# Three more steps of hp in seven products, in chunk 1, and what is moved to make room for them

## The chip, the cores and the metric

The kernel runs on one core of one Trainium2 chip. The metric is the device time of one execution, in microseconds. The core's engines work side by side, each through its own list of instructions in order, and wait for each other through semaphores: TensorE (PE, matrix products into PSUM), VectorE (DVE), ScalarE (ACT), GpSimd (POOL), and SyncE (SP), which starts most of the DMA transfers.

## The reference

Two blocks follow each other. The first is a chunked scan (Mamba-2's SSD) over 4 sequences of 8 heads and 768 positions; the second is a feed-forward layer over the 3072 tokens that come out of it.

```python
# scan: batch 4, heads 8, seq 768, head_dim 32, d_state 16
la = np.log(np.clip(a, 1e-06, 1.0))
for c in range(nc):                         # chunks of positions
    cum = np.cumsum(la[chunk c], axis=-1)
    L = np.exp(cum[..., :, None] - cum[..., None, :]) * causal
    M = np.einsum('bhin,bhjn->bhij', Cc, Bc) * L
    y = np.einsum('bhij,bhjd->bhid', M, xc) \
        + np.einsum('bhin,bhnd->bhid', Cc, state) * np.exp(cum)[..., None]
    state = np.exp(np.sum(la))[..., None, None] * state \
        + np.sum(Bc outer xc * np.exp(cum[..., -1:] - cum), axis=positions)
# feed-forward: x is y as (3072 tokens, 256)
h = x @ w_in                                # 256 -> 2048
g = h * np.cos(h)
out = g @ w_out                             # 2048 -> 256
```

## The kernel before, in words

All data are float32. The 768 positions are cut into NC = 6 chunks of 128 positions; a chunk has 4 x 128 = 512 tokens. The feed-forward layer of chunk c is cut into NF = 16 steps, so that there are 96 steps, n = 16 c + f. A step takes 256 of the 512 tokens (a unit, u = 0 or 1) and 256 of the 2048 features. In step n

- `first(n)` writes hp = x w_in of the step, 512 columns of one PSUM bank, by four products of 128x128 weights with 256 columns (L662);
- `wind_k` (ScalarE, L669) and `wind_w` (VectorE, L675) reduce hp to a fraction of a turn, `gate` (ScalarE, L684) takes the cosine, and `gated` (VectorE, L689) writes gT = hp cos(hp). gT is the last reader of hp;
- from chunk 1 on `differ` (GpSimd, L714, L716, L717) forms the differences gd of gT's four blocks;
- `second(n - 2)` adds the step of two before to the output o. In chunks 1 to 5 that is `seven` (L838): a product of 2x2 blocks by seven block products with 128 columns in place of eight, whose seven sums are taken apart once a unit is through (`rest`, L863, from ps, the copy of o).

`first7` does for hp what `seven` does for o: seven products (L762) in place of four of twice the width. It needs differences of y on GpSimd (`differ_y`, L744, four of them, into the scratch tile ms[2]) and of w_in (`differ_in`, L733, four tiles wid), a copy on ScalarE (L769), and four sums on VectorE (L775, L778, L780, L783). The products are issued in the order 1, 6, 7, 5, 4, 3, 2; product 6 reads the third difference of y, product 4 the fourth. The steps that are done so stand in `runs`: before the change f = 9 to 13 of chunks 2, 3 and 4, and 13 steps of chunk 5. In a run, VectorE and ScalarE work on a step while TensorE makes the next (`late`), and `first_of_seven` picks the PSUM bank of hp:

```python
if i == 0:
    at_["hp"] = pair("hp")[:, 0]
    at_["m"] = pair("m").rearrange("p b (q m) -> p b q m", m=P)
to_ = at_["hp"] if i % 3 == (n > NF * (NC - 1)) else bank([P, TB], "hp", "h")
```

Here i counts the steps of the run, and the step behind the run is counted too. m holds the sums of products that are not in hp's own blocks.

PSUM has 8 banks: two buffers of one bank for "o", two for "h" (hp), and two buffers of two banks each, which `pair` hands out in turn: to the products of C and B (g), to y, and in a run to hp and m. A new holder of a buffer waits until the last reader of the old one is done.

Between the steps of chunk c the scan of chunk c + 1 is made, its parts placed by hand in `steps`, by f: `reach` (running products, L576), `turn` (transposes of B and C on VectorE, L584, then in the next step cT on ScalarE, L593, and rT on VectorE, L595), `inner` (`inner2`: products of C and B into the two g, L605), `weigh` (`weights`: g by the decays lam, on VectorE, L467, which frees g), `state` (`add_state`: the state over a sub-chunk, VectorE, L500), `decays` (running products lam, VectorE, L377, and at the end of each pair sc, GpSimd, L383) and `along` (loads). `open2(c + 1)` multiplies C by the state into two new y tiles (L619) and forms sums (L479); `finish2` adds the products of x (L631) at the end of the chunk. For chunk 2, which is prepared in chunk 1, the places differ from those of the others, since the first chunks are done in another form. There, `add_s` (L553, L560) forms the last state of chunk 1 in that form, and `exchange` (L565) moves quarters of it with four DMAs on SP's queue.

The order of instructions on each engine is the order in which the program issues them; nothing reorders them. In step n it is, in short: hp of step n; on VectorE w of the step; GpSimd's and VectorE's work for the scan; gT; `open2` where it is due; o of step n - 2; `inner2`.

Of the kernel before, what the change touches and what calls it, by code (L numbers as in the profile page):

```python
# [25 lines left out]
def kernel(  # L26
# [18 lines left out]
    NC = S // P  # L45
    DM, DF = moe_w_in.shape
    KT = DM // P
    NF = DF // P
# [23 lines left out]
    def pair(name):  # L72

        return psum.tile([P, 2, 4 * P], FP32, tag="scan", bufs=2, name=name)


    along, blocks = {}, {}
# [54 lines left out]
    def group(q, s):  # L132
        return slice(32 * (q ^ s), 32 * (q ^ s) + 32)
# [223 lines left out]
    reach, part, yT, after = {}, {}, {}, {}  # L357
# [71 lines left out]
    def reach_unit(k):  # L429

        flat = "p b i -> p (b i)"
        V.tensor_tensor_scan(
            out=reachs[k].rearrange(flat), data0=alongs[k].rearrange(flat),
            data1=lead.rearrange(flat), initial=0.0, op0=ALU.mult, op1=ALU.add)
# [35 lines left out]
    def sums(k, at, strip, start=False):  # L470

        sc = scs.pop(k).rearrange("p (q k h) n -> p q k (h n)", q=2, h=2)
        x2 = xrs[k].rearrange("p q (k h) d -> p q k (h d)", h=2)
        for p in range(2):
            for s in range(2):
                ss = slice(s * W, (s + 1) * W)
                for q in range(4):
                    r = strip(q, s)
                    PE.matmul(at[s][r, p * W:(p + 1) * W], lhsT=sc[ss, p, q], rhs=x2[ss, p, q],  # L479
                              start=(start and p == 0), stop=True,  # L480
                              tile_position=(s * W, r.start), skip_group_check=True)
# [131 lines left out]
    def open2(c):  # L613

        ys[c] = y = [pair("y") for _ in range(2)]
        for k, p, s, q in ((k, p, s, q) for k in range(2) for p in range(2) for s in range(2)
                           for q in range(4)):
            r, o_, i = group(q, s), W * (q % 2), (2 * k + p) * W
            PE.matmul(y[s][o_:o_ + W, q // 2, i:i + W], lhsT=after[2 * c + k - 1][r, s, p],  # L619
                      rhs=part[c, s][2][r, p, k * W:(k + 1) * W], start=(k == p == 0), stop=False,  # L620
                      tile_position=(r.start, o_), skip_group_check=True)
        for k in range(2 if c < NC - 1 else 0):
            sums(2 * c + 1 + k, [y[s][:, 0, (2 + k) * P:(3 + k) * P] for s in range(2)], group)
# [21 lines left out]
    NJ = NF // 2  # L645
# [52 lines left out]
    def differ_w(i, js):  # L698

        if i == len(wd):  # L700
            t = conv.tile([P, 2 * WC, 2], U32, tag="words", bufs=8, name="words")
            wd.append(t.rearrange("p a w -> p (a w)").bitcast(FP32)
                      .rearrange("p (j m) -> p j m", j=NJ))
        w11, w12, w21, w22 = (w4[:, js, e, h] for e in range(2) for h in range(2))
        a_ = (w12, w22, w22, w21)[i]
        b_ = (w11, w12, wd[0][:, js], wd[min(i, 2)][:, js])[i]
        op = ALU.add if i in (1, 2) else ALU.subtract
        G.tensor_tensor(out=wd[i][:, js], in0=a_, in1=b_, op=op)  # L708
# [15 lines left out]
    def differ_in(i, js):  # L724

        if i == len(wid):
            t = conv.tile([P, 2 * WC, 2], U32, tag="words", bufs=8, name="wid")
            wid.append(t.rearrange("p a w -> p (a w)").bitcast(FP32)
                       .rearrange("p (j f) -> p j f", j=NJ))
        g = [win4[:, k, js, e] for k in range(2) for e in range(2)]  # L730
        a_ = (g[1], g[1], g[0], g[2])[i]
        b_ = (g[3], g[0], wid[0][:, js], wid[min(i, 2)][:, js])[i]
        G.tensor_tensor(out=wid[i][:, js], in0=a_, in1=b_, op=ALU.subtract)  # L733

    def differ_y(c, i, eng, us=slice(0, 2)):

        if i == 0:
            yd[c] = ms[2].rearrange("p (i u m) -> p i u m", i=4, u=2)
        d = yd[c]
        y11, y12, y21, y22 = (yT[c][:, us, k, h * P:(h + 1) * P] for k in range(2)  # L740
                              for h in range(2))
        a_ = (y12, y22, y22, y21)[i]
        b_ = (y11, y12, d[:, 0, us], d[:, 2, us])[i]
        eng.tensor_tensor(out=d[:, i, us], in0=a_, in1=b_,  # L744
                          op=ALU.add if i in (1, 2) else ALU.subtract)
# [125 lines left out]
    unsummed, finished, summed = [], [], [0]  # L871
# [96 lines left out]
    def rest_of_loads():  # L968
# [21 lines left out]
        for k in (4, 5):  # L990
            for s in range(2):
# [1 line left out]

    steps = {c: dict(reach=(5, 6), turn=(6, 7), inner=8, weigh=(9, 10), state=(-NF, 12),
                     decays=(8, 11, 13, 14), along=(12, 13)) if c == 2 else
             dict(reach=(1, 2), turn=(3, 4), inner=5, weigh=(6, 7), state=(0, 5),
                  decays=(2, 8, 14, 15), along=(6, 7)) for c in range(2, NC)}
    first_decays = (NF + 1, NF + 2, NF + 3, NF + 4)  # L1000
# [11 lines left out]
    def decays2(k, p):  # L1012
        decays0(k, p)
        if p == 1:
# [8 lines left out]

    runs = [*(range(NF * c + 9, NF * c + 14) for c in range(2, NC - 1)),
            range(NC * NF - 15, NC * NF - 2)]
    sevens = {n: r for r in runs for n in r}
    late, at_ = [], {}
# [76 lines left out]
    for n in range(AHEAD, NC * NF + LAG):  # L1106
        c, f = divmod(n, NF)
        if n < NC * NF:
# [64 lines left out]
            if add_s and (n == NF - 5 or units_at(n - 1, 4)):  # L1173
                exchange = add_s()
                add_s = None
            if n == NF + 9:
                exchange()
            for do in behind:
                do()
            if n == runs[-1][0] - 2:  # L1180
                for i in range(4):
                    differ_y(NC - 1, i, V)
            for i, at in enumerate((4, 5, 6, 6) if 2 <= c < NC - 1 else ()):
                if at == f:
                    differ_y(c, i, G, slice(1, 2))
            if unsummed and (c > 1 or summed[0]):
                unsummed[0](range(summed[0], summed[0] + 1), G)
                summed[0] = (summed[0] + 1) % 4
                if summed[0] == 0:
                    unsummed.pop()  # L1190
            elif n not in sevens and f not in ((10, 11, 12) if c == 1 else (10, 11)):
                for do in unsummed:
                    do()
                unsummed.clear()
# [2 lines left out]
                    weigh0(k)  # L1197
        for i, js in differ_at.get(n, ()):
            differ_w(i, js)
        for start, js in zip((2 * NF - 5, 3 * NF - 3, 4 * NF - 3),  # L1200
                             (slice(1, 6), slice(0, 1), slice(6, NJ))):
            if start <= n < start + 4:
                differ_in(n - start, js)
        if f == NF - 2 and 1 < c < NC - 1:
            open2(c + 1)
        if n == AHEAD + 1:
            second(AHEAD - LAG)
# [4 lines left out]
        for k in units_at(n, 3):  # L1212
            for t in range(2):
                inner(k, t)
            if k == 3:
                at = [gs[k, s][:, 0, 2 * P:] for s in range(2)]
# [5 lines left out]
            take_s()  # L1222
        for k in units_at(n, 1):
            reach_unit(k)
        if n == 2 * NF - 3:
            open2(2)
        for at, e in block_loads.items():
            if at == n:
                loading = load_blocks(e)
# [32 lines left out]
```

## Time and profile before

| | |
|---|---|
| runs | 364.67, 366.04, 367.22 us; median 366.04 us |
| the profiled execution | 365.45 us, of it 363.7 us from its first to its last instruction (the span) |
| TensorE | busy 357.1 us (98% of the span), 4070 matmuls, granted clock 1.00 |
| its weight loads | busy 326.1 us (90%) |
| VectorE | busy 275.4 us (76%) |
| GpSimd | busy 237.5 us (65%) |
| ScalarE | busy 184.2 us (51%) |
| the chain that ended last | 92% on TensorE, 3% GpSimd, 2% DMA |

A line of the profile names the source line, the engine, the operation, and the tiles as output<-inputs. In the timeline the first two numbers of a row are its start and its length in microseconds, equal operations that follow each other are merged into one row (x8), and what stands in square brackets at the end is idle time before the row and what ended it. Every float32 product is two matmul instructions. Matmuls overlap, so the time that one costs is read from the starts of rows that follow each other, not from their lengths. The times of the runs and of the profiled execution hold some 2 us that lie outside the span.

### The profile page before, as it was taken

The page shows a single profiled execution, that of the slowest core. Times are in us where ns is not written, and L with a number is a line of the kernel's source. Part 1 is how long each engine was busy: PE and PEld are TensorE (multiplying, and loading weights), DVE is VectorE, ACT ScalarE, POOL GpSimd, SP SyncE. Part 2 cuts the span into 40 slices and gives each one's busy share as a digit, 9 for nine tenths or more (in the row PEclk, how much of TensorE's full clock was granted, in tenths as well). Part 3 has the DMA queues.
Part 4 walks back from the last instruction along what each step waited for, and adds up shares of the span by engine and source line. Part 5 has one row for each costly group of instructions (what it writes and reads, how often), then busy time and mean ns, then how long its engine had stood idle before and what let it go on. Part 6 is the DMA issues. An engine that isn't in the chain of part 4 may idle for free.

```text
span 363.7 us, 10280 instructions
## 1 busy us (share of the span) xinstructions
PE 357.1 (98%) x4070; PEld 326.1 (90%) x4070; DVE 275.4 (76%) x504; ACT 184.2 (51%) x352; POOL 237.5 (65%) x387
## 2 busy tenths in 40 slices
PE   8999999999999999999999999999999999999995
PEld 4688888889899999999989999999999999999995
DVE  7779998478777986877766877775766775688774
ACT  3497656544464345544446543545553544454542
POOL 5557776679757787575685565686666565475562
PEclk9999999999999999999999999999999999999999
DMA  7996947693666427311417202110001001001001
GB/s 138 251 358 151 186 109 120 88 155 58 127 102 90 92 52 115 47 31 45 84 40 123 31 5 67 34 33 13 0 2 31 0 3 32 0 3 31 2 14 46
DMA packets 97328, 26.43 MB, mean 73 GB/s; under 512 B 87328, under 2 KB 93184, under 8 KB 97280
## 3 DMA queue, kind: packets, MB, share of 16 engines
q1 hardware_dynamic: 96032, 25.38, 34.9%
q8 instruction: 32, 0.52, 0.7%
q10 hardware_dynamic: 1248, 0.39, 0.5%
q14 instruction: 16, 0.13, 0.1%
HBM read 22.36 MB, written 3.34 MB: 71 GB/s over the span
## 4 chain that ended last, share of the span: by engine, by line
PE 92%; POOL 3%; DMA 2%; DVE 1%; issue 1%; ACT 0%; POOLq 0%; DVEq 0%; ACTq 0%
PE o L838 34%; PE hp L662 31%; PE m L762 7%; PE o L798 7%; PE hp L762 5%; DMA bc<-in_C_dram 2%; PE y L631 2%; PE g L605 1%; PE y L479 1%; PE y L619 1%; POOL gd L714 1%; PE g L458 1%; POOL words L708 1%; PE y L527 1%; PE y L517 1%
## 5 line engine op out<-in xcount | busy, mean ns | idle before, releaser
L662 PE MATMUL hp<-yT,w_in 128*128 128x256 f32 x544 | 129.5, 382 | 0.1
L662 PEld LDWEIGHTS hp<-yT,w_in 128*128 128x128 f32 x544 | 99.0, 190 | 13.7 <-issue 1.3
L714 POOL TENSOR_TENSOR gd<-gT 128x256 f32<-128x256 f32 x79 | 58.9, 745 | 76.4 <-DVE gT L689 64.2
L684 ACT ACTIVATE w<-w,quarter 128x512 f32<-128x512 f32 x96 | 69.4, 723 | 65.0 <-DVE w L675 64.8
L675 DVE SCALAR_TENSOR_TENSOR w<-hp,k 128x512 f32<-128x512 f32 x96 | 65.7, 685 | 46.6 <-ACT k L669 46.4
L669 ACT ACTIVATE k<-hp 128x512 int32<-128x512 f32 x96 | 57.1, 595 | 69.8 <-PE hp L662 61.0
L689 DVE TENSOR_TENSOR gT<-hp,w 128x512 f32<-128x512 f32 x96 | 65.5, 682 | 11.9 <-ACT w L684 7.4
L838 PE MATMUL o<-words,gd 128*128 128x128 f32 x474 | 66.1, 276 | 0.1
L838 PEld LDWEIGHTS o<-words,gd 128*128 128x128 f32 x474 | 59.3, 192 | 0.3 <-POOL gd L716 0.3
L838 PE MATMUL o<-w_out,gT 128*128 128x128 f32 x316 | 50.3, 278 | 0.0
L838 PEld LDWEIGHTS o<-w_out,gT 128*128 128x128 f32 x316 | 45.4, 191 | 3.1
L716 POOL TENSOR_TENSOR gd<-gT,gd 128x128 f32<-128x128 f32 x79 | 40.5, 512 | 6.2
L717 POOL TENSOR_TENSOR gd<-gT,gd 128x128 f32<-128x128 f32 x79 | 37.3, 472 | 6.2
L838 PE MATMUL o<-w_out,gd 128*128 128x128 f32 x158 | 30.6, 276 | 0.0
L838 PE MATMUL o<-words,gT 128*128 128x128 f32 x158 | 30.5, 275 | 0.0
L798 PE MATMUL o<-w_out,gT 128*128 128x256 f32 x128 | 30.0, 380 | 0.0
L377 DVE TENSOR_TENSOR_SCAN lam<-arow,unit 128x512 f32<-128x512 f32 x20 | 29.6, 1480 | 0.0
L798 PEld LDWEIGHTS o<-w_out,gT 128*128 128x128 f32 x128 | 24.2, 190 | 3.6 <-POOL w_out L273 0.4
L838 PEld LDWEIGHTS o<-words,gT 128*128 128x128 f32 x158 | 24.0, 192 | 0.0
L838 PEld LDWEIGHTS o<-w_out,gd 128*128 128x128 f32 x158 | 24.0, 192 | 0.0
L762 PE MATMUL m<-m,wid 128*128 128x128 f32 x168 | 23.5, 276 | 0.0
L762 PE MATMUL hp<-yT,w_in 128*128 128x128 f32 x112 | 21.6, 275 | 0.0
(130 smaller groups left out, 460.8 us busy)
## 6 DMA issues: line engine op xcount, KB each, us to landing
words<-in_moe_w_in_dram SPq DMA_DIRECT2D x8, 512.0 KB
words<-in_moe_w_out_dram SPq DMA_DIRECT2D x8, 512.0 KB
xr<-in_x_dram SPq DMA_DIRECT2D x24, 128.0 KB
arow<-a_cut SPq DMA_DIRECT2D x10, 256.0 KB
arow<-a_cut SPq DMA_DIRECT2D x10, 252.0 KB
out_dram<-sum SPq DMA_DIRECT2D x18, 128.0 KB
bc<-in_B_dram SPq DMA_DIRECT2D x24, 64.0 KB
blocks<-in_B_dram SPq DMA_DIRECT2D x16, 32.0 KB
```

Of the source, the lines that this page charges most:

```text
L377: V.tensor_tensor_scan(out=lams[k][:, p, hs].rearrange(flat), data0=rows_.rearrange(flat), data1=unit0[:, hs].rearrange(flat), initial=0.0 ...
L662: PE.matmul(to_[:, e], lhsT=w_in[:, k, fs], rhs=y[:, k], start=(k == 0), stop=(k == KT - 1), skip_group_check=True)
L669: ACT.activation(k, hp[n], AF.Copy, bias=0.25, scale=INV_2PI)
L675: V.scalar_tensor_tensor(out=w, in0=hp[n], scalar=INV_2PI, in1=k, op0=ALU.mult, op1=ALU.subtract)
L684: ACT.activation(cos, cos, AF.Sin, bias=quarter, scale=TWO_PI)
L689: V.tensor_tensor(out=gT[n], in0=hp.pop(n), in1=cos, op=ALU.mult)
L714: G.tensor_tensor(out=d[:, 0:2], in0=g[:, 1:2].to_broadcast([P, 2, P]), in1=g[:, 3::-3], op=ALU.subtract)
L716: G.tensor_tensor(out=d[:, 2], in0=g[:, 0], in1=d[:, 0], op=ALU.subtract)
L717: G.tensor_tensor(out=d[:, 3], in0=g[:, 2], in1=d[:, 2], op=ALU.subtract)
L762: PE.matmul(dst[q], lhsT=w[q], rhs=y_[q], start=(q in (6, 1, 7)), stop=True, skip_group_check=True)
L798: PE.matmul(o[c, u][:, t], lhsT=g[:, 2 * e + t], rhs=w_out[:, 2 * j + e], start=(j == e == t == 0), stop=(j == NJ - 1 and e == 1), skip_gr ...
L838: PE.matmul(at[q], lhsT=a_[q], rhs=w[q], start=(j == 0 and q in starts), stop=(j == NJ - 1), skip_group_check=True)
```

## The change

- `runs` gets a run of three steps in chunk 1: n = 27, 28, 29 (f = 11 to 13). The four differences of y of chunk 1 are formed on GpSimd in steps 24, 25 and 26 (f = 8, 9, 10, 10).
- The differences of w_in, which all stood behind step 26, are cut otherwise: columns 3 to 5 in steps 22, 22, 24 and 25; 1 and 2 in steps 30 to 33; 0 and 6 to 7 as before.
- `open2(2)`, the state times C, moves from the end of step 29 (behind o of step 27) to step 30, between hp of step 30 and o of step 28, where the other chunks have it.
- The sums of unit 0 of chunk 1 (L863), which were four operations on VectorE in one step, become one on GpSimd in each step of the run and the one behind it.
- In `steps` of chunk 2: `state` (-16, 12) becomes (-16, 10), and `decays` (8, 11, 13, 14) becomes (7, 8, 14, 15). With the decays, the loads of arow and sc (L383) that hang on them move.
- `exchange()` moves from step 25 to step 24.

```diff
-    steps = {c: dict(reach=(5, 6), turn=(6, 7), inner=8, weigh=(9, 10), state=(-NF, 12),
-                     decays=(8, 11, 13, 14), along=(12, 13)) if c == 2 else
+    steps = {c: dict(reach=(5, 6), turn=(6, 7), inner=8, weigh=(9, 10), state=(-NF, 10),
+                     decays=(7, 8, 14, 15), along=(12, 13)) if c == 2 else
...
-    runs = [*(range(NF * c + 9, NF * c + 14) for c in range(2, NC - 1)),
+    runs = [range(NF + 11, NF + 14), *(range(NF * c + 9, NF * c + 14) for c in range(2, NC - 1)),
             range(NC * NF - 15, NC * NF - 2)]
...
-            if n == NF + 9:
+            if n == NF + 8:
                 exchange()
...
-            for i, at in enumerate((4, 5, 6, 6) if 2 <= c < NC - 1 else ()):
+            for i, at in enumerate((8, 9, 10, 10) if c == 1 else (4, 5, 6, 6) if 2 <= c < NC - 1
+                                   else ()):
                 if at == f:
                     differ_y(c, i, G, slice(1, 2))
-            if unsummed and (c > 1 or summed[0]):
+            if unsummed and (c > 1 or n in sevens or summed[0]):
                 unsummed[0](range(summed[0], summed[0] + 1), G)
...
-        for start, js in zip((2 * NF - 5, 3 * NF - 3, 4 * NF - 3),
-                             (slice(1, 6), slice(0, 1), slice(6, NJ))):
-            if start <= n < start + 4:
-                differ_in(n - start, js)
-        if f == NF - 2 and 1 < c < NC - 1:
+        for at, js in (((22, 22, 24, 25), slice(3, 6)), ((30, 31, 32, 33), slice(1, 3)),
+                       ((45, 46, 47, 48), slice(0, 1)), ((61, 62, 63, 64), slice(6, NJ))):
+            for i, m in enumerate(at):
+                if m == n:
+                    differ_in(i, js)
+        if f == NF - 2 and 1 <= c < NC - 1:
             open2(c + 1)
...
-        if n == 2 * NF - 3:
-            open2(2)
```

## The prediction

> **What bounds the kernel now.** I read the engine totals and the chain that ended last first, then the timeline engine by engine round the edited steps, and last the same steps of the next chunk, which already run in the new form.
>
> ```profile
> PE 357.1 (98%) x4070; PEld 326.1 (90%) x4070; DVE 275.4 (76%) x504; ACT 184.2 (51%) x352; POOL 237.5 (65%) x387
> PE 92%; POOL 3%; DMA 2%; DVE 1%; issue 1%; ACT 0%; POOLq 0%; DVEq 0%; ACTq 0%
> ```
>
> TensorE is busy for 357.1 of 363.7 us and is 92% of the chain. No stage has slack to give back: a microsecond in which TensorE waits is a microsecond at the end, and one that it saves is gained only if nobody else is late.
>
> The TensorE timeline of steps 27 to 30 (chunk 1), and then of two seven-product steps and step 46 (chunk 2):
>
> ```profile
> 115.54 1.89 PE L662 MATMUL hp<-yT,w_in 128*128 128x256 f32 x8
> 117.27 0.61 PE L838 MATMUL o<-w_out,gT 128*128 128x128 f32 x4
> ...
> 118.83 1.89 PE L662 MATMUL hp<-yT,w_in 128*128 128x256 f32 x8
> ...
> 125.51 0.94 PE L619 MATMUL y<-rT,state 32*64 32x64 f32 x64
> ...
> 176.01 0.39 PE L762 MATMUL hp<-yT,w_in 128*128 128x128 f32 x2
> ...
> 179.14 0.39 PE L762 MATMUL hp<-yT,w_in 128*128 128x128 f32 x2
> ...
> 182.26 1.89 PE L662 MATMUL hp<-yT,w_in 128*128 128x256 f32 x8
> 184.09 0.91 PE L619 MATMUL y<-rT,state 32*64 32x64 f32 x64
> ```
>
> The reader sees that hp by four products costs 1.73 us (115.54 to 117.27) of a step of 3.29 (115.54 to 118.83), that a step with seven products lasts 3.13 (176.01 to 179.14), and that in chunk 2 the state products (L619) follow the hp of step 46 without idle.
>
> VectorE behind that hp of step 46, and GpSimd ahead of step 25:
>
> ```profile
> 186.07 0.68 DVE L675 SCALAR_TENSOR_TENSOR w<-hp,k 128x512 f32<-128x512 f32 x1
> 186.67 1.44 DVE L377 TENSOR_TENSOR_SCAN lam<-arow,unit 128x512 f32<-128x512 f32 x1
> 188.03 0.66 DVE L689 TENSOR_TENSOR gT<-hp,w 128x512 f32<-128x512 f32 x1
> ...
> 112.34 0.73 POOL L714 TENSOR_TENSOR gd<-gT 128x256 f32<-128x256 f32 x1
> ```
>
> gT of step 46 is done at 188.69, 4.6 us after TensorE was through with that step's hp at 184.09. Nobody waits for it there. GpSimd begins gd of step 24 at 112.34.
>
> **What the edit saves.** Steps 27, 28 and 29 take 3.13 instead of 3.29 us: 3 x 0.16 = **-0.5 us**. That is all it can bring. The sums of unit 0 leave VectorE (127.49 to 130.99 before, L863), where nothing on TensorE's path waited for them, and become four GpSimd operations of 0.73, 0.73, 0.73 and 0.46 us (the rows from 175.33 on), each behind a gd, with 0.6 us and more idle after it in chunk 2: 0. The three L769 copies (0.27 each) and three times four VectorE sums (0.29, 0.41, 0.43, 0.29) fit as they do in chunk 2: 0, and uncovered 1.7 us a step.
>
> **A wait at step 30: the state products.** `pair` hands out two PSUM buffers in turn. After the change they go to the two g of step 24, then to hp and m of the run (step 27), then to the two y of `open2`, which now stands behind hp of step 30 and ahead of o of step 28. `first_of_seven` puts hp into the pair's bank whenever i % 3 is 0. With five steps in a run (chunks 2 to 4) that is f = 9 and 12, long consumed at f = 14. With three steps it is step 27 and, as i = 3, step 30 itself. So the second y takes the buffer in which hp of step 30 has just been written, and in the built program its first product waits for VectorE's count after gT of step 30, hp's last reader. Before gT come k, w, cos on ScalarE and VectorE, those of step 29 ahead of them, and the lam scan of step 30, which stands between w and gT as in step 46. The nearest row is therefore step 46 itself: 188.69 - 184.09 = **+4.6 us** in which TensorE has nothing in front of it but the rest of `open2`; o of step 28 and hp of step 31 are queued behind. Low end: step 25, whose k, w and cos find their engines free: hp ends at 110.69 (108.86 + 1.83), gT at 113.82 (113.13 + 0.69), 3.1. High end: the scan collides with GpSimd as at 131.59, where it took 2.45 instead of 1.37 us: 4.6 + 1.1 = 5.7.
>
> ```profile
> 131.41 1.56 POOL L733 TENSOR_TENSOR wid<-w_in,wid 128x640 f32<-128x640 f32 x1
> ...
> 131.59 2.45 DVE L377 TENSOR_TENSOR_SCAN lam<-arow,unit 128x512 f32<-128x512 f32 x1
> ```
>
> **A wait at step 27: the differences of y.** The second product of step 27 (q = 6) needs the third difference of `differ_y`, on GpSimd in step 26. From 112.34 on GpSimd's order is now: sc of L383, moved here from 120.22 (0.64); gd of step 24 (112.34 to 114.11, 1.77); a difference of y (0.46, 0.5 with the gap); wid of 384 columns (between 0.73 for 256 and 1.54 for 640, a line through them gives 1.0, with gap 1.05); gd of step 25 (1.8); y (0.5); wid (1.05); y (0.5), the one that is needed. Sum 7.8, so 120.1. Without a wait the product would start at 115.54 + 0.22 = 115.76: 4.4 late. GpSimd may reach this chain sooner, since gT of step 23 now runs ahead of the transposes (0.7), and L717 of that step, 1.25 us at 108.87 beside the scan, may take its usual 0.46: 1.5 together, so 2.9 late. I take **+3.8**, nearer to the row as it stands, because the scan still meets GpSimd, with another operation. The two wid operations put into step 22 (2.1 us) fall into GpSimd's idle time of 104.11 to 107.46.
>
> VectorE gives the floor. The scan and gT of step 23 (108.40 to 110.40, 2.0 us) now stand ahead of the transposes, of which the second used to wait for its DMA until 106.14. So the transposes end at about 107.7 instead of 106.80, cT on ScalarE is 0.9 later, and the products of `inner2`, which began on it at 107.78, wait as long. Hp of step 26 and w follow 0.9 later, and the two `weights` that free the g buffers now run together behind w of step 26 (114.87 before): 114.87 + 0.9 + 0.6 + 2 x 0.6 = 117.6, 1.8 after 115.76. These waits run beside GpSimd's, so they are not added but are the low end: +1.8. If they ran one behind the other, 0.9 + 4.4 = 5.3.
>
> The exchange (L565) is issued a step earlier and `add_state` two steps earlier. L560 ended at 112.39 before and `add_state` begins near 118, so the four transfers of 16 KB have some 5 us; SP's queue has two arow loads ahead of them that wait for nothing late. `add_state` (four L500, 2.37 us) now lies between `weights` and the sums of step 27, inside TensorE's wait: 0, and 2.4 if that wait is gone.
>
> **Clock.** A gap of 4.6 us is longer than any that this trace has between matmuls (the longest after the first 10 us is 0.74). After the last matmul, which ended at 359.9, the granted clock is still 1.00 in the last row, up to 363.7:
>
> ```profile
> 362.00:363.70 1.70, 0.00 (x0) 0.00 (x0) 0.00 (x0) 0.00 (x0) 0.00 (x0) 1.00 0.08 18
> ```
>
> So 3.8 us of idleness did not lower it. (The columns are the stretch, its length, the busy time of the five engines, the granted clock, and two of DMA.) What a lowered clock would cost is bounded by the kernel's start:
>
> ```profile
> 3.46 2.56 PE L366 MATMUL a_ps<-m 128*128 128x256 f32 x6
> ```
>
> A pass of 256 columns took 0.43 us there (2.56 / 6) against 0.22 later, for about 5 us: half of that, 2.5. I take 0, with 2.5 as the high end. [...]
>
> **Sum.** -0.5 + 4.6 + 3.8 = +7.9. The profiled execution took 365.45 us (span 363.7), so 373.35; the median of the runs, 366.04, lies 0.6 above it. I say 373.5.
>
> **Rivals.** (1) *GpSimd keeps up*, and step 27 waits for VectorE alone: 365.45 - 0.5 + 4.6 + 1.8 = 371.35. For it: 1.5 us of GpSimd's delays may go, and VectorE's part is bounded; against it: 7.8 us of GpSimd work in a row. (2) *The clock falls* in the gap of step 30: 373.4 + 2.5 = 375.9. For it: the gap exceeds the 3.8 us that are shown harmless; against it: by 0.8 alone. (3) *The other side: chunk 1 runs as chunk 2 does.* gT of step 30 is done when TensorE comes to `open2`, GpSimd's differences too, and only the 0.5 us shows: 364.9. For it: five such steps at 166.48 to 182.26 without idle. It decides once gT of step 30 ends within 0.5 us after its hp; the least that any row gives is 3.1 us, and the buffer is the same one.
>
> **How the numbers follow.** Forecast 0.50, (1) 0.20, (2) 0.26, (3) 0.02, other 0.02. The lowest sum of bounds is 365.45 - 0.5 + 3.1 + 1.8 = 369.85; the highest without the clock is 365.45 - 0.5 + 5.7 + 5.3 = 375.95, with it 378.5. The range 369.9 to 377.0 leaves out (3) and the far end of (2). About 1% (3.7 us) is what a measurement of this kernel tells from no change; even the lowest sum is 4.4 above, so faster by over 1%: 0.01, within: 0.04, slower: 0.95.
>
> **What would show it.** Right: an idle gap of 3 to 5.7 us on TensorE inside L619, ended by gT of L689; a gap of 2 to 4 us ahead of the L762 products of step 27, ended by L744; 0.9 us inside L605; steps of 3.13 behind them. Wrong: L619 back to back with hp of step 30, or the first L762 products without a wait. A PEclk under 9 behind 130 us speaks for (2).

## The result, and the profile after

The changed kernel takes **375.64 us** (median of 6 runs, 374.0 to 376.4) where the kernel before, run beside it, takes 366.94 (6 runs, 364.67 to 369.18). The ratio is 1.0257, 95% interval 1.0221 to 1.0292: 2.6% slower, or 9.4 us on 366. The profiled execution took 375.98 us, one of the longer runs; its span is 374.2 (363.7 before).

From the page of the changed kernel, the engine totals, the granted clock in 40 slices of 9.4 us, and the chain that ended last:

```profile
PE 360.4 (96%) x4088; PEld 329.1 (88%) x4088; DVE 275.0 (73%) x512; ACT 185.1 (49%) x355; POOL 245.2 (66%) x399
...
PEclk9999999999998989999999999999999999999999
...
PE 87%; POOL 8%; issue 2%; DVE 1%; ACT 0%; POOLq 0%; DVEq 0%; ACTq 0%
```

TensorE is no longer busy nearly all the time: its busy time grew by 3.3 us, the span by 10.5, so most of the growth is idleness. GpSimd's share of the chain went from 3% to 8%. The clock shows two notches ahead of and behind 130 us, where the line before was all nines.

The TensorE timeline of the changed kernel, steps 24 to 31 (columns as before; the bracket is idle time and what ended it):

```profile
103.57 1.89 PE L662 MATMUL hp<-yT,w_in 128*128 128x256 f32 x8
...
108.46 1.14 PE L605 MATMUL g<-cT,turned 32*64 32x128 f32 x56 [1.06 <-ACT cT L593]
109.53 1.99 PE L662 MATMUL hp<-yT,w_in 128*128 128x256 f32 x8
...
112.92 1.89 PE L662 MATMUL hp<-yT,w_in 128*128 128x256 f32 x8
...
116.89 0.49 PE L762 MATMUL hp<-yT,w_in 128*128 128x128 f32 x2 [0.51 <-DVE m L467]
119.13 1.43 PE L762 MATMUL m<-m,wid 128*128 128x128 f32 x6 [1.75 <-POOL m L744]
...
121.63 1.06 PE L838 MATMUL o<-w_out,gT 128*128 128x128 f32 x4
...
123.76 0.39 PE L762 MATMUL hp<-yT,w_in 128*128 128x128 f32 x2
123.99 0.83 PE L762 MATMUL m<-m,wid 128*128 128x128 f32 x6
...
125.33 0.61 PE L838 MATMUL o<-w_out,gT 128*128 128x128 f32 x4
...
126.89 0.39 PE L762 MATMUL hp<-yT,w_in 128*128 128x128 f32 x2
...
130.02 1.89 PE L662 MATMUL hp<-yT,w_in 128*128 128x256 f32 x8
131.84 0.34 PE L619 MATMUL y<-rT,state 32*64 32x64 f32 x8
136.52 1.21 PE L619 MATMUL y<-rT,state 32*64 32x64 f32 x56 [4.34 <-issue]
...
138.78 1.22 PE L838 MATMUL o<-w_out,gT 128*128 128x128 f32 x4
...
140.95 1.89 PE L662 MATMUL hp<-yT,w_in 128*128 128x256 f32 x8
```

Three stops are seen: inside L605, ahead of and behind the first product of step 27, and inside L619 after 8 of 64 products, where the first y is done and the second needs its buffer. Steps 28 and 29 run without a stop and last 3.13 us each (123.76 to 126.89 to 130.02). Two stretches are slow without being stops: the six products of step 27 take 2.50 us (119.13 to 121.63), those of step 28 only 1.34 (123.99 to 125.33); and the rows behind L619's stop are longer too. The granted clock by stretches tells why (stretch, length, busy time of PE, PEld, DVE, ACT and POOL, clock, DMA):

```profile
116.00:119.40 3.40, 1.14 (x8) 0.75 (x7) 3.35 (x7) 0.99 (x2) 3.16 (x7) 1.00 0.50 55
119.40:122.82 3.42, 3.42 (x18) 3.42 (x18) 1.59 (x4) 0.00 (x0) 0.27 (x1) 0.50 0.25 53
122.82:126.00 3.18, 3.18 (x31) 3.18 (x31) 1.20 (x5) 0.77 (x2) 2.33 (x4) 1.00 0.16 42
133.06:136.47 3.41, 0.00 (x0) 0.00 (x0) 3.22 (x4) 1.24 (x3) 2.55 (x4) 1.00 0.00 0
136.47:139.89 3.42, 3.37 (x125) 3.12 (x126) 0.00 (x0) 0.00 (x0) 2.90 (x7) 0.50 0.03 5
```

Twice a stretch of 3.4 us ran at half the clock (0.50), each time just behind a stretch in which TensorE had mostly or wholly stood still (busy for 1.14 of 3.40 us and for 0.00 of 3.41). The idle stretch itself still shows 1.00.

Who ends the stops, from VectorE's and GpSimd's timelines of the same kernel:

```profile
103.84 2.02 DVE L377 TENSOR_TENSOR_SCAN lam<-arow,unit 128x512 f32<-128x512 f32 x1
...
134.41 1.43 DVE L377 TENSOR_TENSOR_SCAN lam<-arow,unit 128x512 f32<-128x512 f32 x1
135.76 0.66 DVE L689 TENSOR_TENSOR gT<-hp,w 128x512 f32<-128x512 f32 x1
...
103.51 3.15 POOL L733 TENSOR_TENSOR wid<-w_in 128x384 f32<-128x384 f32 x2
...
112.37 0.73 POOL L714 TENSOR_TENSOR gd<-gT 128x256 f32<-128x256 f32 x1
...
118.62 1.05 POOL L744 TENSOR_TENSOR m<-yT,m 128x128 f32<-128x128 f32 x2
```

gT of step 30 ends at 136.42, and the second y goes on at 136.52. The profile names no releaser there ("issue"); that it is gT's release of hp's buffer is shown by the first experiment. The third difference of y is the first of the two L744 at 118.62; it is done at about 119.1, and product 6, the first of the six L762, starts at 119.13.

**The account**, from hp of step 24 to hp of step 31: 103.57 to 140.95 is 37.38 us, against 26.32 before (104.24 to 130.56): +11.06. By its parts:

| part | how it is read | us |
|---|---|---|
| three steps shorter | 3 x (3.13 - 3.29) | -0.5 |
| step 24 with L605 | 5.96 (103.57 to 109.53), before 4.62 (104.24 to 108.86) | +1.34 |
| stops in step 27 | product 6 at 119.13; from hp of step 26 it was due at 112.92 + 3.29 + 0.22 = 116.43 | +2.70 |
| half clock, first stretch | six products 2.50, not 1.34; o of step 25 2.13 (to 123.76), not 1.56 | +1.73 |
| stop inside L619 | 131.84 to 138.78 is 6.94; in chunk 2 of the same kernel 1.63; less 0.74 of slow products | +4.57 |
| half clock, second stretch | the products behind the stop 2.26, not 1.52; o of step 28 2.17, not 1.66 | +1.25 |
| sum | | +11.09 |

The span grew by less, 10.5, because step 24 began 0.67 us earlier in this execution. The ratio of the runs stands for 9.4, not 10.5: the account is that of one execution.

### The profile page after: what moved, and what is told of

It reads as the page before. It is cut to its first block, busy times and chain, and to the rows that moved or that the text cites. A ratio compares the mean times of both kernels' runs of the same rounds, so it can differ in the third digit from the quotient of the medians.

```text
span 374.2 us, 10340 instructions
## 1 busy us (share of the span) xinstructions
PE 360.4 (96%) x4088; PEld 329.1 (88%) x4088; DVE 275.0 (73%) x512; ACT 185.1 (49%) x355; POOL 245.2 (66%) x399
## 4 chain that ended last, share of the span: by engine, by line
PE 87%; POOL 8%; issue 2%; DVE 1%; ACT 0%; POOLq 0%; DVEq 0%; ACTq 0%
PE o L838 31%; PE hp L662 27%; PE m L762 8%; PE o L798 7%; PE hp L762 6%; POOL gd L714 2%; PE y L631 2%; POOL wid L733 1%; POOL gd L716 1%; PE y L619 1%; POOL words L708 1%; PE y L479 1%; POOL gd L717 1%; PE g L605 1%; POOL sc L383 1%
## 5 line engine op out<-in xcount | busy, mean ns | idle before, releaser
L662 PE MATMUL hp<-yT,w_in 128*128 128x256 f32 x520 | 123.8, 382 | 0.1
L662 PEld LDWEIGHTS hp<-yT,w_in 128*128 128x128 f32 x520 | 94.6, 190 | 13.1 <-issue 1.3
L838 PE MATMUL o<-w_out,gT 128*128 128x128 f32 x316 | 51.4, 282 | 0.0
L762 PE MATMUL m<-m,wid 128*128 128x128 f32 x186 | 26.5, 280 | 1.8 <-POOL m L744 1.8
L762 PEld LDWEIGHTS m<-m,wid 128*128 128x128 f32 x186 | 23.6, 195 | 2.0 <-POOL m L744 1.9
L775 DVE TENSOR_TENSOR m<-m 128x128 f32<-128x128 f32 x31 | 9.0, 292 | 21.5 <-PE m L762 18.0
L762 PE MATMUL hp<-yT,w_in 128*128 128x128 f32 x124 | 24.3, 278 | 0.5 <-DVE m L467 0.5
```

The lines of the kernel that those rows point to most:

```text
L662: PE.matmul(to_[:, e], lhsT=w_in[:, k, fs], rhs=y[:, k], start=(k == 0), stop=(k == KT - 1), skip_group_check=True)
L762: PE.matmul(dst[q], lhsT=w[q], rhs=y_[q], start=(q in (6, 1, 7)), stop=True, skip_group_check=True)
L838: PE.matmul(at[q], lhsT=a_[q], rhs=w[q], start=(j == 0 and q in starts), stop=(j == NJ - 1), skip_group_check=True)
```

## The experiments

All start from the changed kernel. Each ratio is to the kernel before, run on the same chip, with its 95% interval in brackets. Theory going in: the whole loss is TensorE's stops, each a named wait, plus half-clock stretches that the stops bring on. Rivals: the seven-product form or its sums on GpSimd have a price of their own in chunk 1; or one stop alone decides and the others are covered by it.

**e1: hp of step 30 in a bank of "h".**

```diff
-        to_ = at_["hp"] if i % 3 == (n > NF * (NC - 1)) else bank([P, TB], "hp", "h")
+        to_ = (at_["hp"] if i % 3 == (n > NF * (NC - 1)) and n != 2 * NF - 2 else
+               bank([P, TB], "hp", "h"))
```

> Theory (the second y waits for gT of step 30, because hp of that step lies in the pair's buffer): with hp of step 30 in a bank of h, that wait (4.6 us in the changed kernel) is gone, and so is the half-clock window behind it (1.4 us). In exchange hp of step 30 waits for gT of step 28, which frees that bank: gT ended at 130.72 where hp began at 130.02, so 0.7 us. The time falls by 5.3 us from the changed kernel's, to about 370.3; TensorE shows no gap inside L619. Rival (TensorE is held by the late VectorE and GpSimd, and L619 is only where it shows): the gap reappears within two steps at an o or an hp, and the time falls by less than 1.5 us.

370.75 us, the median of four runs (369.1 to 375.28), ratio without the longest of them 1.0124 [1.0086, 1.0163]. The TensorE timeline of e1 at step 30:

```profile
130.97 1.97 PE L662 MATMUL hp<-yT,w_in 128*128 128x256 f32 x8 [0.68 <-DVE gT L689]
132.86 0.91 PE L619 MATMUL y<-rT,state 32*64 32x64 f32 x64
```

All 64 state products stand in one row behind hp: the stop is gone, and a wait of 0.68 for the bank of "h" stands ahead of hp in its place. One line of the source is worth 4.9 of the 9.4 us that the ratio of the change stands for. So the stop was the buffer of the pair, and nothing else that the change does at step 30.

Up to step 29 e1 has the same instructions as the change, and yet its profile differs there: 1.88 us of idle time inside L605 in place of 1.06, a half-clock stretch behind it, and 0.90 in place of 1.75 ahead of product 6. How the stops of steps 24 to 27 divide differs from one execution to the next, which matters for e2 and e8.

**e2: wid earlier.** GpSimd's wid of 384 columns in steps 20, 21, 22, 22.

```diff
-        for at, js in (((22, 22, 24, 25), slice(3, 6)), ((30, 31, 32, 33), slice(1, 3)),
+        for at, js in (((20, 21, 22, 22), slice(3, 6)), ((30, 31, 32, 33), slice(1, 3)),
```

> The four differences of w_in for the run stand in steps 20, 21, 22 and 22 in place of 22, 22, 24 and 25, so two of 1.0 us leave the stretch of GpSimd ahead of step 27. Theory (step 27 waits for GpSimd's queue): the third difference of y is done 2 us sooner, product 6 of step 27 waits until VectorE's part ends, 117.4 in place of 119.1; 1.7 us less of waiting, and the half-clock window behind it (1.7 us) is gone too, since the gap falls to some 0.5 us: 3.4 us less, 372.2. Rival (VectorE's weights and the state sums are what step 27 waits for): the gap ahead of L762 stays above 1.5 us and the time within 1 us of 375.6.

376.18 us, ratio 1.0282 [1.0246, 1.0318]: no gain at all. The TensorE timeline of e2:

```profile
108.94 1.99 PE L605 MATMUL g<-cT,turned 32*64 32x128 f32 x56 [2.11 <-ACT cT L593]
...
119.48 0.91 PE L762 MATMUL m<-m,wid 128*128 128x128 f32 x6 [0.20 <-DVE m L467]
```

The wait for GpSimd is gone (0.20, and ended by VectorE), but the stop inside L605 is 2.11 instead of 1.06: in this execution the second transpose waited 0.88 us for the DMA of its blocks as well. The clock fell behind that stop, and hp of step 25 took 2.41 us. That this stop grew is not shown to be the edit's doing, since e1 has 1.88 there without it. What e2 shows is that VectorE's L467 is the next to end the wait ahead of product 6, and that the time of the four runs did not fall. The state's exchange, which the prediction had left at nothing, shows as well: L500 waited 1.43 us for it.

**e3: the scan behind the transposes**, as before the change, all else as changed.

```diff
-                     decays=(7, 8, 14, 15), along=(12, 13)) if c == 2 else
+                     decays=(8, 8, 14, 15), along=(12, 13)) if c == 2 else
```

> The first lam scan of the next chunk moves from step 23 to step 24, behind the transposes (decays 8, 8, 14, 15 in place of 7, 8, 14, 15). Theory: the wait inside L605 (1.06 us) goes to about 0.1, but GpSimd's sc and gd of step 24 still follow the scans, so product 6 of step 27 begins about when it did, and the time stays within 1 us of the changed kernel's 375.6. Rival (the waits follow each other, and each is paid): 1.3 us less, 374.3.

378.5 us, ratio 1.0352 [1.0319, 1.0385]: slower than the change, where none of the expectations had it. The TensorE timeline of e3 at product 6:

```profile
120.70 1.65 PE L762 MATMUL m<-m,wid 128*128 128x128 f32 x6 [3.95 <-POOL m L744]
```

gT of step 23 stands behind the transposes again, so that GpSimd begins gd of that step at 107.50, 0.9 us later than in the change (106.62). The second sc (0.64) falls behind gd of step 24. (The second scan also meets GpSimd's L553, 1.67 us for the pair in place of 0.76, but the first sc is as much shorter, 0.63 in place of 1.55.) So GpSimd's chain, and with it product 6, is 1.6 us later, and two half-clock stretches follow in place of one, by the stretches of e3:

```profile
119.49:122.90 3.41, 2.20 (x10) 2.20 (x11) 0.01 (x1) 0.00 (x0) 1.61 (x3) 0.50 0.98 86
122.90:126.31 3.41, 3.41 (x18) 3.41 (x18) 1.93 (x5) 0.00 (x0) 1.25 (x3) 0.50 0.10 22
```

Here it is GpSimd's queue that sets step 27. The stop inside L605 shrank only to 0.84, since the blocks of C landed at 106.1.

**e4: TensorE kept busy in step 30.** Five products that nobody reads, ahead of the state products.

```diff
+        if c == 2:
+            for _ in range(5):
+                PE.matmul(y[0][:, 0], lhsT=w_in[:, 0, 0:P], rhs=w_in[:, 0, 0:4 * P],
+                          start=True, stop=True, skip_group_check=True)
```

> Five products of 128x512 that nobody reads are put ahead of the state products of chunk 2, into the first y tile, whose buffer is free by then: 10 passes of some 0.43 us, 4.3 us, about as long as TensorE waits there. Theory (the idle gap lowers the clock for one window of 3.4 us, and the work in it takes twice as long): the clock stays 1.00 behind step 30, the state products and o behind them run at full speed, and the time falls by 1.4 us although work was added, to 374.2. Rival (the slow window has to do with something else than idleness, or costs nothing): the clock falls all the same and the time is the same or longer by up to 0.5 us.

373.83 us, ratio 1.0235 [1.0196, 1.0274]. The timeline of e4 (its line numbers are 4 higher from here on):

```profile
129.84 4.45 PE L618 MATMUL y<-w_in 128*128 128x512 f32 x10
134.22 1.23 PE L623 MATMUL y<-rT,state 32*64 32x64 f32 x64
135.38 0.86 PE L479 MATMUL y<-xr,sc 64*32 64x64 f32 x64
136.17 0.71 PE L842 MATMUL o<-w_out,gT 128*128 128x128 f32 x4
137.83 1.89 PE L666 MATMUL hp<-yT,w_in 128*128 128x256 f32 x8
```

o of step 28 takes 1.66 (136.17 to 137.83), not the 2.17 of the change: 4.4 us of useless work cost nothing, and the clock was 1.00 from 134.42 to 141.25, where the change has its second stretch at 0.50. That is read from the profile; the times of e4 and of the change are not told apart by their intervals. Less expected was that the clock did not fall in step 27 either, with the same stops as in the change (0.51 and 1.75):

```profile
116.77:120.19 3.42, 1.67 (x14) 1.48 (x15) 1.86 (x4) 0.27 (x1) 2.48 (x5) 1.00 0.64 96
120.19:123.60 3.41, 3.41 (x33) 3.41 (x32) 2.53 (x9) 0.86 (x2) 1.09 (x2) 1.00 0.48 52
```

So the same stops, 2.26 us together (0.51 + 1.75), had a half-clock stretch behind them in the change and none in e4; the last section sets the two stretches beside each other. The spread of the change's runs fits: 374.0 and 374.12 at mean clocks of 0.994 and 0.995, and 375.3 to 376.4 at 0.989 to 0.991, where the profiled execution, with its two such stretches, has 0.991.

**e5: all stops out.** The bank (the pair's only for i = 1), the scan behind the transposes, wid in steps 20 to 22, and the differences of y on VectorE in steps 24 and 25.

```diff
-                     decays=(7, 8, 14, 15), along=(12, 13)) if c == 2 else
+                     decays=(8, 8, 14, 15), along=(12, 13)) if c == 2 else
...
-        to_ = at_["hp"] if i % 3 == (n > NF * (NC - 1)) else bank([P, TB], "hp", "h")
+        in_pair = i == 1 if n < 2 * NF else i % 3 == (n > NF * (NC - 1))
+        to_ = at_["hp"] if in_pair else bank([P, TB], "hp", "h")
...
-            for i, at in enumerate((8, 9, 10, 10) if c == 1 else ...
-                    differ_y(c, i, G, slice(1, 2))
+            for i, at in enumerate((8, 8, 9, 9) if c == 1 else ...
+                    differ_y(c, i, V if c == 1 else G, slice(1, 2))
...
-        for at, js in (((22, 22, 24, 25), slice(3, 6)), ...
+        for at, js in (((20, 21, 22, 22), slice(3, 6)), ...
```

> All three waits are taken away at once, each at its cause: hp of step 28 (not 27 and 30) in the pair's bank, so that open2 takes a buffer whose reader is done; the scan behind the transposes; the differences of w_in in steps 20 to 22; the differences of y on VectorE in steps 24 and 25, off GpSimd's queue. Theory (the lost time is those three waits and the slow clock behind them): what stays is up to 0.8 us inside L605 for the DMA of the transposes and up to 0.5 us for the weights ahead of step 27, against the 0.5 us saved; no half-clock window; 365.5 to 367 where before takes 366. Rival (seven products in chunk 1 overload VectorE or GpSimd as such): the waits come back at other places and the time stays over 369.

366.13 us (before 365.78), ratio 1.0022 [1.0001, 1.0043]. One stop is left:

```profile
117.33 0.94 PE L762 MATMUL m<-m,wid 128*128 128x128 f32 x6 [1.47 <-DVE m L467]
```

The run, its sums on GpSimd, the moved state, scan and exchange are all still there, and the time is that of before but for this stop: 1.47 - 0.5 = +1.0, where the ratio says +0.8. That leaves no room for a price of the form itself beyond some 1 us (the interval is 0.8 us either way).

**e6: the moves without the run** (no run and no differences of y in chunk 1).

```diff
-    runs = [range(NF + 11, NF + 14), *(range(NF * c + 9, NF * c + 14) for c in range(2, NC - 1)),
+    runs = [*(range(NF * c + 9, NF * c + 14) for c in range(2, NC - 1)),
...
-            for i, at in enumerate((8, 9, 10, 10) if c == 1 else (4, 5, 6, 6) if 2 <= c < NC - 1
-                                   else ()):
+            for i, at in enumerate((4, 5, 6, 6) if 2 <= c < NC - 1 else ()):
```

> The changed kernel without the run of chunk 1 (27 to 29 by four products, the differences of y of chunk 1 left out as nobody reads them); the moves of decays, state, exchange, open2 and w_in stay. Theory: what the moves cost by themselves is the wait inside L605, 1.1 to 2.1 us with the landing of the DMA, and now and then a half-clock window (1.7 us): 367.0 to 369.5 where before takes 366. Rival (the moves are free without the run): within 0.5 us of before.

367.45 us, ratio 1.0052 [1.0034, 1.007], so +1.9. Its profile, of the fastest of the ten runs, has one stop, the one inside L605:

```profile
108.70 1.14 PE L605 MATMUL g<-cT,turned 32*64 32x128 f32 x56 [1.06 <-ACT cT L593]
```

Step 24 is 1.34 us longer than before by this stop, as in the change. That lies inside the interval of the 1.9 (1.2 to 2.6); three of the ten runs had a mean clock of 0.994.

**e7: the run without the moves** (`decays`, `state` and `exchange` as before the change; the pair's bank for i = 1 only, as in e5; the differences of w_in and `open2` stay where the change puts them).

```diff
-    steps = {c: dict(reach=(5, 6), turn=(6, 7), inner=8, weigh=(9, 10), state=(-NF, 10),
-                     decays=(7, 8, 14, 15), along=(12, 13)) if c == 2 else
+    steps = {c: dict(reach=(5, 6), turn=(6, 7), inner=8, weigh=(9, 10), state=(-NF, 12),
+                     decays=(8, 11, 13, 14), along=(12, 13)) if c == 2 else
...
-            if n == NF + 8:
+            if n == NF + 9:
                 exchange()
```

> The run of three steps with the differences it needs, and the places of decays (8, 11, 13, 14), state (-16, 12) and exchange (25) as before the change; hp of step 28 in the pair's bank. Theory: no wait inside L605 beyond 0.1 to 0.8 us; GpSimd has one sc less ahead of step 27, so product 6 waits some 3 us where it waited 4; then the scan of step 27 and the state sums of step 28 lie between the sums of the run on VectorE, 1.4 and 2.0 us more than its 0.5 us a step of slack, so 2 to 3 us more of waiting in steps 28 to 30: 370 to 372 where before takes 366. Rival (the moves are what costs, the run is nearly free): under 368.

369.21 us, ratio 1.0103 [1.0071, 1.0135], less than expected. One stop, of the size expected, and one half-clock stretch behind it:

```profile
118.43 1.51 PE L762 MATMUL m<-m,wid 128*128 128x128 f32 x6 [2.92 <-POOL m L744]
```

The scan and the state inside the run bring no stop of their own here, where 2 to 3 us were expected. With step 27 so late this says little of the scan; e10 says more.

**e8: only the differences of y on VectorE.** The `differ_y` edit of e5 alone.

```diff
-            for i, at in enumerate((8, 9, 10, 10) if c == 1 else ...
-                    differ_y(c, i, G, slice(1, 2))
+            for i, at in enumerate((8, 8, 9, 9) if c == 1 else ...
+                    differ_y(c, i, V if c == 1 else G, slice(1, 2))
```

> The changed kernel with the four differences of y of chunk 1 on VectorE in steps 24 and 25 instead of on GpSimd in steps 24 to 26, and nothing else. Theory (GpSimd's queue holds step 27): the 1.75 us ahead of product 6 fall to 0.5 or less, since VectorE had 2.0 us of idle time at 110.3; the wait inside L605 and the 4.6 us at L619 stay. 1.3 to 3.4 us less than the changed kernel's 375.6 (the second figure where the half-clock window goes too): 372.2 to 374.3. Rival (step 27 waits for VectorE's weights and sums all the same): no gain, 375 or more.

375.18 us, ratio 1.026 [1.0234, 1.0287]: a miss of the same kind as e2. GpSimd's wait is gone, and what is left ahead of step 27 is ended by VectorE's L467 (0.93 and 0.20), as the rival had it. The stop inside L605 is 1.89 in this execution, with a half-clock stretch behind it, as in e1. Behind the untouched stop of L619 there are two such stretches in a row, as the clock by stretches of e8 shows:

```profile
131.01:134.42 3.41, 0.92 (x12) 0.43 (x10) 2.17 (x4) 1.71 (x4) 2.56 (x5) 1.00 0.11 31
134.42:137.83 3.41, 1.56 (x88) 1.47 (x89) 1.75 (x2) 0.57 (x1) 3.10 (x6) 0.50 0.03 8
137.83:141.25 3.42, 3.42 (x68) 3.25 (x49) 0.00 (x0) 0.00 (x0) 1.45 (x4) 0.50 0.32 75
141.25:144.60 3.35, 3.35 (x139) 2.86 (x138) 0.51 (x1) 0.60 (x1) 0.00 (x0) 1.00 0.63 132
```

The stop fell across two stretches, each more than half idle, and each is followed by one at 0.50.

The last three look for a version that beats the kernel before, and put the theory to its sharpest test: is the time nothing but the sum of the stops in the timeline, less the 0.5 us that the run saves?

**e9: e5, with the first two differences of y on GpSimd again and the last two L467 ahead of VectorE's differences.**

```diff
-                     inner=8, weigh=(9, 10)
+                     inner=8, weigh=(9, 9)
...
-                    differ_y(c, i, V if c == 1 else G, slice(1, 2))
+                    differ_y(c, i, V if c == 1 and i > 1 else G, slice(1, 2))
```

> All of the change with the waits taken out as in e5_all_waits_out, and two further edits against its last wait (1.47 us ahead of the six L762 products of step 27, ended by VectorE's L467): the first two differences of y of chunk 1 go back to GpSimd, in step 24, and the last two L467 are put ahead of the VectorE differences. VectorE then has 0.8 us less ahead of the L467 that is waited for. Own theory (TensorE's waits and nothing else make the time): the wait falls to 0.7 us or less and the time to 0.8 to 1.2 us under e5's 366.13, thus 364.9 to 365.4, 0.1% to 0.2% under the kernel before. Rival (a fixed price of the run or of its sums): it stays at 366.

367.08 us (before 366.38), ratio 1.0033 [1.0006, 1.0061]. The stop that was aimed at shrank as expected, and another came behind it:

```profile
116.47 0.94 PE L762 MATMUL m<-m,wid 128*128 128x128 f32 x6 [0.50 <-DVE m L744]
...
118.70 0.49 PE L762 MATMUL hp<-yT,wid 128*128 128x128 f32 x2 [1.02 <-ACT m L769]
```

**e10: e7, with GpSimd's wid in steps 20 to 22 and its differences of y in steps 24 and 25** (f = 8, 8, 9, 9). Against e7:

```diff
-            for i, at in enumerate((8, 9, 10, 10) if c == 1 else ...
+            for i, at in enumerate((8, 8, 9, 9) if c == 1 else ...
...
-        for at, js in (((22, 22, 24, 25), slice(3, 6)), ...
+        for at, js in (((20, 21, 22, 22), slice(3, 6)), ...
```

> The run alone as in e7_run_alone (scan, state times and exchange where they were before; the pair's bank for i = 1 only), with GpSimd's work for step 27 earlier: the wid operations in steps 20 to 22 and the differences of y in steps 24 and 25, all still on GpSimd. Own theory: the 2.92 us wait ahead of the six L762 products of step 27 falls to some 0.7 (VectorE's two L467, which ended at 116.34 there, stay), the half-clock window goes with it, and 369.2 becomes 365.0 to 366.0: no slower than before. If wid in steps 20 to 22 delays the transposes here too (e2_wid_early), a wait of about 1 us inside L605 comes in its place and the time is 366.5 to 368. Rival (the seven-product form costs time in chunk 1 whatever waits): 368 or more.

366.49 us, ratio 1.0017 [0.9997, 1.0037]: not to be told from the kernel before. TensorE's two stops in e10 (no half-clock stretch follows), and what stands behind the second on VectorE and GpSimd:

```profile
116.09 0.94 PE L762 MATMUL m<-m,wid 128*128 128x128 f32 x6 [0.66 <-POOL m L744]
...
121.67 0.94 PE L838 MATMUL o<-words,gd 128*128 128x128 f32 x6 [0.40 <-POOL gd L716]
...
119.35 1.22 DVE L377 TENSOR_TENSOR_SCAN lam<-arow,unit 128x512 f32<-128x512 f32 x1
...
119.38 1.70 POOL L714 TENSOR_TENSOR gd<-gT 128x256 f32<-128x256 f32 x1 [2.81 <-PE o L838]
```

The second stop is the price of the scan that is left in step 27: GpSimd's gd of step 26 meets it and takes 1.70 us in place of 0.73. e11 has the same stop; e5 and e9, with the scan moved ahead of the run, have none there. So that move does serve the run once step 27 is in time. The order of e10 on GpSimd with the scan moved was not run.

**e11: e7, with the four differences of y on VectorE** (f = 8, 8, 9, 9), that is, with the edit of e8.

> The run alone as in e7_run_alone, with the four differences of y of chunk 1 on VectorE in steps 24 and 25 instead of GpSimd; wid stays where the change puts it. Own theory: L467 and the differences end on VectorE at about 117 (2.2 us more work in queue, some 1.8 us of idle time there to take it), so the wait ahead of the six L762 products is 1 to 1.8 us instead of 2.92, without a half-clock window in most executions: 366 to 367.5. Rival (only GpSimd's load counts, VectorE's does not): 365.3, no wait.

367.31 us, ratio 1.0038 [1.001, 1.0065]. Stops of 1.50 (ahead of product 6, ended by L467) and 0.40 us (as in e10); 0.21 us more in step 32.

| kernel | stops of 0.2 us and more, steps 24 to 31 | less 0.5 | measured, from the ratio (x 366) |
|---|---|---|---|
| e5 | 1.47 | +1.0 | +0.8 |
| e9 | 0.50 + 1.02 | +1.0 | +1.2 |
| e10 | 0.66 + 0.40 | +0.6 | +0.6 |
| e11 | 1.50 + 0.40 | +1.4 | +1.4 |

Without half-clock stretches in the profile, the stops alone give the time within 0.2 us. That is closer than the evidence allows, and partly luck: the intervals are about 1 us either way, and the brackets leave out some 0.2 us a stop (by the starts of rows, from hp of step 24 to hp of step 31, e5, e9, e10 and e11 are 1.7, 1.6, 1.2 and 1.8 us longer than the kernel before, and shorter elsewhere). By either reading no price of the form of much over 1 us is left. No version tried beats the kernel before; e10 comes nearest. Its two waits of together 1.06 us, both for GpSimd, would have to go below 0.5 for that.

## Why the prediction was right or wrong

**Direction, and the wait at step 30: right, in place, size and cause.** Predicted 4.6 us inside L619, ended by gT with the lam scan ahead of it; measured 4.57, with the scan at 134.41 to 135.8 between w and gT. The price came from chunk 2, where the same stretch was harmless because nobody waited for it. e1 shows the cause.

**The wait at step 27: right in sum, less so in its parts.** Predicted 3.8 from the unstalled start of product 6 to its real one; measured 1.34 + 2.70 = 4.04. The chain on GpSimd from gd of step 24 (112.37) to the third difference (119.1) is the one predicted, with wid at the 1.0 us that was interpolated. That the sum came so near is partly luck. It was taken under 4.4 because GpSimd might reach the chain up to 1.5 us sooner; counted from hp of step 24 it did not (8.20 us, 111.77 - 103.57, where the row before gave 8.10), but the chain took 7.4 us in place of 7.8. That VectorE's wait runs beside GpSimd's and is not added fits e2 and e8: product 6 waited for L467 there in place of GpSimd, and the time did not fall. A cost was missed: the two wid in step 22 were to fall into GpSimd's idle time, but met VectorE's scan of step 23, which took 2.02 us in place of some 1.4, and the wait inside L605, foreseen at 0.9, is 1.34. One mark failed: the gap ended by L744 is 1.75, not 2 to 4, because 1.06 at L605 and 0.51 for L467 had already been spent ahead of it.

**The saving, and what was put at nothing.** Steps of 3.13 came as predicted, and the table above closes with the 0.5. Sums on GpSimd and `add_state` brought no stop (e5, e7). The exchange was covered with little to spare: VectorE waited for it for 0.82 us in e1 and 1.43 in e2.

**The clock: wrong, and nearly the whole of the miss.** The step that failed is "3.8 us of idleness did not lower it. (...) I take 0". It read the last row of the kernel before, clock 1.00 up to the end of the span, as a sign that idleness of that length is harmless. The stretches of the changed kernel show that such a row can't tell: the idle stretch itself (133.06 to 136.47, TensorE 0.00) carries 1.00, and the half clock comes in the one behind it. In e4 the last product ends at 366.89, 3.8 us before the end of the span as well, and there the fall still lies inside the span, in its last row:

```profile
369.36:370.66 1.30, 0.00 (x0) 0.00 (x0) 0.00 (x0) 0.00 (x0) 0.00 (x0) 0.50 0.00 0
```

In the kernel before it came at 364.0, just behind the end of the span at 363.7.

Measured: 1.73 + 1.25 = 3.0 us, where 0 was taken and 2.5 was the high end. The waits and the saving come to 8.1 where 7.9 was predicted, so what the forecast lacked is the clock. (375.64 lies only 2.1 above 373.5, since the profiled span grew by 0.6 us less than the account of its steps, and the median is a little under the profiled run.) Rival (2), 375.9, had the mechanism at step 30. That its sum came so near is partly luck: the stretch behind that gap cost 1.25, not 2.5, and a second stretch, which it did not have, cost 1.73 behind the shorter stops of step 27.

The 2.5 us came from passes of 0.43 us at the start of the kernel before. The stretches show a granted clock of 1.00 there too (0.00 to 5.00), so that a lowered clock as the cause of those passes was the author's estimate; no view shows it. The clock also fell behind stops shorter than the 3.8 us that were taken as harmless: 0.51 and 1.75 us in the change, and 2.92 us in e7.

## What to carry to other kernels

Before part of a pipeline is copied to another place, follow each rotating buffer through the new order: a rule that is harmless in a run of five steps (every third step takes the pair's bank) put the run's last hp, in a run of three, into the buffer that the next stage needed at once, and cost half of the loss. On a TensorE that is busy 98% of the time, a stop may have to be priced with a half-clock stretch behind it: here none followed single stops of 1.06 to 1.50 us (e6, e5, e11), one followed those of 1.88 us (e1) and more, and the two of the change cost 1.7 and 1.3 us (the next section has the rows). When several engines are late by similar amounts, the removal of one wait proves little; take all of them out at once first, then put them back one by one.

## What was not expected of the hardware

A stretch need not be wholly idle for the clock to fall. In the change the granted clock changes at 119.41, 122.82, 136.47 and 139.89, so the times between the changes are one, four and one times 3.413 us. The table has stretches of this length, counted on from a change of the same profile, at a clock of 1.00:

| run, stretch | TensorE busy, us | clock behind it |
|---|---|---|
| e8, 107.12 to 110.53 | 1.52 | 0.50 |
| e1, 106.11 to 109.52 | 1.53 | 0.50 |
| e2, 105.24 to 108.65 | 1.59 | 0.50 |
| e3, 133.14 to 136.55 | 1.65 | 1.00 |
| e4, 116.77 to 120.19 | 1.67 | 1.00 |

Busy is what the profile counts, with modelled ends. Ahead of other falls TensorE was busy for less: 0.00 and 1.14 us in the change, 0.49 in e3 (116.08 to 119.49), 0.50 in e7 and 0.92 in e8. Counted so from 10 us to the last matmul, every other stretch at 1.00 of the kernel before and of the change had TensorE busy for 1.85 us or more, and none of them had a fall behind it. As an estimate from these rows and from the 3.41 us, a single stop of up to 3.41 - 1.6 = 1.8 us on a TensorE that is otherwise busy leaves no stretch with less than 1.6 us, one of twice that, 3.6, leaves one such stretch however it lies, and between the two it depends on how the stop lies against the edges. That fits the stops seen: none of 1.06 to 1.50 us by itself had a fall behind it, those of 1.88 (e1), 1.89 (e8), 2.11 (e2) and 2.92 us (e7) had, and the same two stops of step 27 left TensorE busy for 1.14 us of one stretch in the change and for 1.67 in e4. Behind stretches that were themselves at 0.50 the clock stayed there with TensorE busy for 1.56 us (e8) and 2.20 us (e3), and was 1.00 again with 3.42 and 3.37 us (the change). What lies between was not shown.

VectorE's scan and GpSimd's wid were both longer where they met: the scan took 2.02 us beside wid and 1.43 without it, the two wid 3.15 us where later ones take 1.0 each (at 103.84, 134.41 and 103.51 in the timelines). The first wid ends at 104.78, the scan 1.1 us later at 105.86, and the second wid, which began at 104.74, ends 0.8 us after that.
